# Banks of PSUM taken in the order given back, and a tick's masks placed ahead of its scores, in a sparse-attention and mixture-of-experts kernel

## The chip, the cores and the metric

The kernel runs on one core of one Trainium2 chip. The metric is the device time of one execution in microseconds (us). Three runs of the kernel before took 524.56, 526.11 and 528.07 us, so the median is 526.11 us.

## What is computed

Block-sparse attention (4 batches, 8 heads, 768 positions, 64 wide, blocks of 32) is followed by a mixture of 8 experts that sends every token to one expert. Cut to the core:

```python
scores = scale * np.matmul(q, k.transpose(0, 1, 3, 2))
mask = np.abs(blk_i - blk_j) <= 1                      # neighbours
mask |= first or last block, as a row or as a column   # dense rows and shared columns
mask |= three sampled blocks for each row of blocks
attn = softmax(np.where(mask, scores, -1e9))
x = (attn @ v) as (3072 tokens, 512)
logits = x @ w_gate + modality_bias[modality_id]
e_idx, gate_w = argmax(logits), softmax(logits) at e_idx
out[tokens of e] = gate_w * (relu(x @ w1[e]) @ w2[e])
```

## The kernel before, in words

The attention is cut into items. A dense item `("d", b, pr)` is the first and last block of queries of one batch and one pair of heads against all 24 blocks of keys. A sparse item `("s", half, m, n, b)` is one block of queries of one batch and all heads against 8 blocks of keys. There are 16 dense and 88 sparse items.

Every item passes through steps, each named by a letter: S scores (TensorE; `dense_scores`, L386, and `scores`, L536, which makes the scores of two sparse items, one for each batch), M maximum and mask (VectorE; `dense_max`, L399 and L400, and `masked`, L544), X exponential (ScalarE; L408, L409, L552), T transposes (TensorE; L418, L561), A copy of the transposes out of PSUM (mostly ScalarE; L425, L566), W and V the weighing of the values (TensorE; L437 for dense, L583 the shared blocks, L592 the own blocks; `sum_rows`, L576, the sums of the exponentials), O the division (VectorE; L444 to L446, L454), Y transposes of a finished tile of 128 tokens (L599, copied by ScalarE in L601) and G the gate (TensorE L609, read by VectorE in L612).

The loop runs in ticks. In tick t a step takes the item t minus the step's `LAG`; within a tick the steps are written out in the order of the string `ORDER`. Between the steps `hook(0)` to `hook(7)` put in other work: loads on SP's queue, copies of keys on GpSimd, routing on VectorE, and the first two groups of experts (`early_groups`). All five engines follow the order in which this code is written. In the first 14 ticks a list of tokens (`START`) sets it instead. After the attention, from about 237 us on, groups of 256 tokens run through the experts (`first_layer` L776 to L778, `second_layer` L791 to L793).

PSUM has 8 banks of 128 x 512 f32. Each result of TensorE takes one by calling `bank()`. Before, the pool handed them out in rotation: the n-th call gets the bank of call n - 8, and TensorE's first write to it waits until the last reader of that earlier holder is done. A holder lives for a very different time: the transposes of T until the copy two statements on, the bank of W from W over V to the last instruction of O, and the two banks of `scores` over the masks of two ticks.

Of the kernel before, what the change touches and what calls it, by code (L numbers as in the profile page):

```python
# [60 lines left out]
ORDER = 'OXTSMGVAYW'  # L61
# [28 lines left out]
def attention_moe(ctx, tc, kD, qD, qH, v0, v1, blocks, modality, w_gate, bias, w1, w2, out):  # L90
# [33 lines left out]
    with ExitStack() as actx:  # L124
# [3 lines left out]
        psum = actx.enter_context(tc.tile_pool(name="psum", bufs=8, space=PSUM))  # L128

        def bank():  # L130
            return psum.tile([P, 512], F32, name="bank")
# [81 lines left out]
        for _ in range(WARM):  # L213
            nc.tensor.matmul(warm[:, 0:P], lhsT=onesb, rhs=onesb, start=True, stop=True)

# [120 lines left out]
        def rank(t0_, t1_):  # L336
# [15 lines left out]
            nc.vector.tensor_tensor(cnt, cnt, rk[:, 256:256 + E], ALU.add)  # L352
            yield
# [25 lines left out]
        def dense_scores(b, pr):  # L379
            q = qd[b // HB]  # L380
            s1, s2 = zip(*[(bank(), bank()[:, 0:256]) for _ in range(2)])
            for o, blocks_ in ((s1, slice(0, 16)), (s2, slice(16, 24))):
                for c in range(2):
                    for u in range(2):
                        r, col = slice(64 * u, 64 * u + 64), 64 * (u ^ c)
                        nc.tensor.matmul(o[c][col:col + 64, :], lhsT=q[r, b % HB * NPAIR + pr + c], rhs=kd[b][r, pr // 2, blocks_, c * 32:c * 32 + 32],  # L386
                                         start=True, stop=True, tile_position=(64 * u, col))
            return zip(s1, s2)
# [8 lines left out]
        def dense_max(b, pr, s1, s2):  # L397
            nm2 = small.tile([P, 2], F32, name="nm2")
            nc.vector.tensor_reduce(nm2[:, 0:1], s1, axis=AX.X, op=ALU.max, negate=True)  # L399
            nc.vector.tensor_reduce(nm2[:, 1:2], s2, axis=AX.X, op=ALU.max, negate=True)  # L400
            nb_ = small.tile([P, 1], F32, name="nb_")
            nc.vector.tensor_scalar(nb_, nm2[:, 0:1], nm2[:, 1:2], 0.125, ALU.min, ALU.mult)
            return s1, s2, nb_

        def dense_exp(b, pr, s1, s2, nb_):
            a = work.tile([P, 768], F32, name="a", bufs=5)
            sm = small.tile([P, 2], F32, name="sm", bufs=6)
            nc.scalar.activation(a[:, 0:512], s1, AF.Exp, bias=nb_, scale=0.125, accum_out=sm[:, 0:1])  # L408
            nc.scalar.activation(a[:, 512:768], s2, AF.Exp, bias=nb_, scale=0.125, accum_out=sm[:, 1:2])  # L409
            return a, sm  # L410
# [10 lines left out]
        def dense_copy(b, pr, tps, sm):  # L421
            at = ad[0]
            ad.append(ad.pop(0))
            for k0, k1, tp in tps:
                (nc.vector.tensor_copy if (b, pr) in DENSE_DVE else nc.scalar.copy)(at[:, k0:k1, :].rearrange("p a b -> p (a b)"), tp[:, 0:(k1 - k0) * P])  # L425
            rt = small.tile([P, 1], F32, name="su", bufs=6)
            nc.vector.tensor_scalar(rt, sm[:, 0:1], sm[:, 1:2], 1e-9, ALU.add, ALU.add)
            nc.vector.reciprocal(rt, rt)
            return at, rt
# [19 lines left out]
        def dense_out(b, pr, o, rt):  # L449
            for u in range(2):  # L450
                col = 64 * (u ^ pr % 2)
                r = slice(col, col + 64)
                dst = xrs[-1, b // HB][64 * (b % HB):64 * (b % HB) + 64, (2 * pr + u) * D:(2 * pr + u + 1) * D]
                nc.vector.tensor_scalar(dst, o[r, 0:D], rt[r], None, ALU.mult)  # L454

# [84 lines left out]
        def masked(m, n, b, sp):  # L540
            y = work.tile([P, 512], F32, name="y", bufs=3).rearrange("p (u k) -> p u k", u=2)
            mn = small.tile([P, 2], F32, name="mn", bufs=4)
            for u in range(2):
                nc.vector.tensor_tensor_reduce(  # L544
                    y[:, u, :].rearrange("p (s f) -> p s f", s=8), sp[u][:, b * 256:(b + 1) * 256].rearrange("p (s f) -> p s f", s=8),
                    smask[:, 2 * m + 1 + n, :].unsqueeze(2).broadcast_to([P, 8, 32]), -0.125, 3.0e38, ALU.add, ALU.min, mn[:, u:u + 1])
            return y, mn
# [16 lines left out]
        def copied(n, b, tp, at):  # L564
            eng = nc.vector.tensor_copy if 2 * n + b in EVAC_DVE else nc.scalar.copy
            eng(at[:, :, n, :], tp.rearrange("p (x q) -> p x q", q=32))  # L566

# [28 lines left out]
        def turned(xr):  # L596
# [4 lines left out]
            nc.scalar.copy(xT.rearrange("p r t -> p (r t)"), tp)  # L601
            return xT

        def gate(tau, xT):
# [7 lines left out]
            nc.vector.tensor_tensor(lgs[tau - tau % 2][:, tau % 2, :], tp[:, 0:E], btok[:, tau, :], ALU.add)  # L612

# [189 lines left out]
        def early_groups():  # L803
# [21 lines left out]
            def columns(g):  # L825
                for n in range(2):
                    if now["column"] == 2 * g + n and now["gather"] > g:
                        column(g, n, bank())
# [20 lines left out]
            for k in range(4):  # L849
# [6 lines left out]
                relu(k, o)  # L856
            o = [bank() for _ in range(2)]
# [11 lines left out]
            for t in range(2):  # L869
                give(0, t, o[t])  # L870
            while now["column"] < 4:
# [9 lines left out]
            for k in range(4):  # L881
                relu(k, o[k])
            o = [bank() for _ in range(2)]
# [8 lines left out]
            for t in range(2):  # L892
                give(1, t, o[t])
            while not ready[2]:
# [5 lines left out]
            piece_numbers(bank())  # L900
# [129 lines left out]
        def choose(i):  # L1030
# [54 lines left out]
            yield from rows_of(tp, 2, gi_e[i], si_e[i])  # L1085
            ready[i] = True
# [8 lines left out]
        def finish():  # L1095
# [69 lines left out]
            yield from rows_of(tp, NCOL, gi, si, False)  # L1165
            ready[NEAR] = True
# [104 lines left out]
        def do(op, it):  # L1271
# [29 lines left out]
            else:  # L1301
# [20 lines left out]
                elif (n, b) == (1, HB - 1):  # L1322
# [7 lines left out]
                    elif op == "O":  # L1330
                        new_tile(m, half)
                        divide(st.pop(it), banks.pop((m, half))[:, 0:H], slice(0, P), H, xrs[m, half])
# [44 lines left out]
        hp, op, xp = [bank() for _ in range(4)], [bank() for _ in range(2)], [bank() for _ in range(2)]  # L1377
# [57 lines left out]
```

## Time and profile before

| | |
|---|---|
| median of 3 runs | 526.11 us |
| profiled execution, device time | 527.7 us |
| its span in the profile | 526.0 us |
| TensorE busy (matmuls) | 499.9 us, 95% |
| VectorE busy | 390.6 us, 74% |
| ScalarE busy | 341.0 us, 65% |
| GpSimd busy | 300.9 us, 57% |

In the profile PE is TensorE, PEld its weight loads, DVE is VectorE, ACT is ScalarE, POOL is GpSimd and SP the engine whose queue issues most transfers. Each row of a timeline gives the start in us from the span's start, the duration in us, then the engine, the line, the operation, what it writes and reads, and the number of instructions merged in it; a bracket at the end says how long the engine was idle before and what ended that. The 1.7 us between 526.0 and 527.7 lie outside of the instructions.

### The profile page before, as it was taken

To read this page: it belongs to the slowest core of one execution; us is meant where nothing else is said; L and a number is where in the kernel's file an instruction comes from. 1 tells how busy PE (TensorE), PEld (TensorE's weight loads), DVE (VectorE), ACT (ScalarE), POOL (GpSimd) and SP (SyncE) were. 2 spreads that over 40 slices of the span, in tenths; PEclk is the share of its full clock that TensorE was granted. 3 is DMA by queue.
4 is the path that set the end of the run, shared out by engine and by line. 5 is a ranking of instruction groups with operands and counts; after the bars stand their busy time and mean duration, and the time that the engine had idled before them with its cause. 6 is when DMAs were issued, how large, how long until landed. Compare 5 with 4: busy or idle time off the path is not lost.

```text
span 526.0 us, 18869 instructions
## 1 busy us (share of the span) xinstructions
PE 499.9 (95%) x7170; PEld 419.7 (80%) x7170; DVE 390.6 (74%) x1125; ACT 341.0 (65%) x777; POOL 300.9 (57%) x534
## 2 busy tenths in 40 slices
PE   7899898998999999889999999999999999999994
PEld 5577676776777777679898998989989899898983
DVE  7875776777877989975995757696776967869671
ACT  3679786886987998961564545464654646546471
POOL 3558763865466888454348742654746548465412
PEclk9989999998999999999999999999999999999997
DMA  7985987868855668968478884857759577585750
GB/s 279 326 232 156 227 248 240 244 175 255 217 178 151 190 203 242 267 195 273 160 242 304 294 272 148 304 184 264 261 183 306 179 259 254 194 305 186 263 196 23
DMA packets 49698, 119.40 MB, mean 227 GB/s; under 512 B 8512, under 2 KB 8896, under 8 KB 49600
## 3 DMA queue, kind: packets, MB, share of 16 engines
q1 hardware_dynamic: 44656, 105.00, 64.4%
q0 software_dynamic: 4944, 13.11, 6.7%
q8 instruction: 58, 0.95, 0.8%
q14 instruction: 40, 0.33, 0.2%
HBM read 105.50 MB, written 12.85 MB: 225 GB/s over the span
## 4 chain that ended last, share of the span: by engine, by line
PE 69%; DMA 14%; DVE 6%; SPq 5%; issue 3%; ACT 2%; POOL 1%; POOLq 0%; DVEq 0%; ACTq 0%
PE bank L776 8%; PE bank L778 8%; PE bank L777 8%; PE bank L793 7%; PE bank L792 7%; PE bank L791 7%; DMA slot<-x_d,gq 6%; PE bank L536 6%; PE bank L561 5%; PE bank L592 3%; PE bank L583 2%; DMA slot<-v 2%; DMA slot<-w 2%; DMA slot<-kD 2%; PE bank L609 2%
## 5 line engine op out<-in xcount | busy, mean ns | idle before, releaser
L728 DVE TENSOR_TENSOR slot<-slot 128x1024 fp32r<-128x1024 f32 x96 | 114.8, 1225 | 45.2 <-ACT slot L724 45.0
L748 POOL DMA_INDIRECT slot<-x_d,gq x72 | 94.5, 1313 | 76.3 <-DVE slot L755 57.0
L724 ACT CAST slot<-slot 128x1024 fp32r<-128x1024 f32 x104 | 106.3, 1047 | 40.0 <-PE bank L777 30.3
L776 PE MATMUL bank<-slot 128*128 128x256 f32 x384 | 107.2, 279 | 0.0
L777 PE MATMUL bank<-slot 128*128 128x256 f32 x384 | 106.3, 277 | 0.0
L778 PE MATMUL bank<-slot 128*128 128x256 f32 x384 | 106.3, 277 | 0.0
L552 ACT ACTIVATE a<-y,mn 128x256 f32<-128x256 f32 x176 | 88.8, 514 | 5.3 <-DVE mn L544 4.5
L793 PE MATMUL bank<-slot 128*128 128x512 f32 x200 | 78.9, 395 | 0.0
L792 PE MATMUL bank<-slot 128*128 128x512 f32 x200 | 78.7, 393 | 0.1
L791 PE MATMUL bank<-slot 128*128 128x512 f32 x200 | 78.4, 392 | 0.0
L777 PEld LDWEIGHTS bank<-slot 128*128 128x128 f32 x384 | 72.3, 188 | 0.4
L776 PEld LDWEIGHTS bank<-slot 128*128 128x128 f32 x384 | 72.1, 188 | 0.6
L778 PEld LDWEIGHTS bank<-slot 128*128 128x128 f32 x384 | 72.1, 188 | 0.0
L544 DVE CUSTOM_DVE_ANT_1 y<-bank,smask 128x256 f32<-128x256 f32 x176 | 66.4, 416 | 3.4 <-PE bank L536 3.0
L484 POOL COPY slot<-slot 128x128 f32 x264 | 64.9, 296 | 0.0
L566 ACT COPY at<-bank 128x512 f32<-128x512 f32 x88 | 50.8, 579 | 9.4 <-PE bank L561 9.4
L506 POOL TENSOR_SCALAR slot<-slot 32x1024 f32<-32x1024 f32 x40 | 41.8, 1045 | 25.6 <-issue 10.8
L561 PE MATMUL bank<-ident,a 128*128 128x128 f32 x352 | 53.2, 284 | 2.5 <-issue 2.5
L536 PE MATMUL bank<-slot,q_raw 64*32 64x256 f32 x1408 | 50.5, 387 | 2.1 <-DMA q_raw<-qH 1.9
L783 ACT ACTIVATE slot<-bank 128x512 fp32r<-128x512 f32 x48 | 28.7, 598 | 35.3 <-PE bank L778 32.5
L784 DVE SCALAR_TENSOR_TENSOR slot<-bank,slot 128x512 fp32r<-128x512 f32 x48 | 32.3, 690 | 20.5 <-ACT slot L783 20.5
L792 PEld LDWEIGHTS bank<-slot 128*128 128x128 f32 x200 | 37.6, 188 | 8.9 <-DVE slot L728 0.8
(299 smaller groups left out, 869.6 us busy)
## 6 DMA issues: line engine op xcount, KB each, us to landing
slot<-w SPq DMA_DIRECT2D x105, 512.0 KB, 5.4
slot<-v SPq DMA_DIRECT2D x180, 128.0 KB, 4.0
q_raw<-qH SPq DMA_DIRECT2D x22, 256.0 KB, 4.5
x_d<-xr SPq DMA_DIRECT2D x22, 256.0 KB, 3.5
slot<-v SPq DMA_DIRECT2D x16, 256.0 KB, 4.9
slot<-kD SPq DMA_DIRECT2D x13, 256.0 KB, 4.4
slot<-v SPq DMA_DIRECT2D x4, 768.0 KB, 13.2
slot<-kD SPq DMA_DIRECT2D x3, 768.0 KB
```

What stands on the lines that cost most here:

```text
L536: nc.tensor.matmul(sp[u][32 * pr:32 * pr + 32, b * 256:(b + 1) * 256], lhsT=q[r, b * NPAIR + pr, n, :], rhs=kv[r, s0:s0 + 8, b, pr, :], st ...
L552: nc.scalar.activation(a[:, u, :], y[:, u, :], AF.Exp, bias=mn[:, u:u + 1], scale=-1.0, accum_out=total[:, u:u + 1])
L561: nc.tensor.transpose(tp[:, k:k + P], a[:, u, c * P:(c + 1) * P], ident)
L724: nc.scalar.copy(h, staged(n))
L728: eng.tensor_tensor(l[:, k:k + size], staged(n)[:, k:k + size], h[:, k:k + size].bitcast(F32), ALU.subtract)
L748: nc.gpsimd.indirect_dma_start(out=xq[0][:, 4 * t + k, :], out_offset=None, in_=table, in_offset=bass.IndirectOffsetOnAxis(ap=gq[:, k, 2 * ...
L776: nc.tensor.matmul(o, lhsT=h[:, fs], rhs=xh[g % 2][:, c, :], start=c == 0 and f % 2 == 0, stop=False)
L777: nc.tensor.matmul(o, lhsT=h[:, fs], rhs=xl[g % 2][:, c, :], start=False, stop=False)
L778: nc.tensor.matmul(o, lhsT=l[:, fs], rhs=xh[g % 2][:, c, :], start=False, stop=c == 3 and f % 2 == 1)
L791: nc.tensor.matmul(o, lhsT=hh[0][:, f, ts_], rhs=h[:, fs], start=f == 0, stop=False)
L792: nc.tensor.matmul(o, lhsT=hh[0][:, f, ts_], rhs=l[:, fs], start=False, stop=False)
L793: nc.tensor.matmul(o, lhsT=hl[f // 4][:, f % 4, ts_], rhs=h[:, fs], start=False, stop=f == 7)
```

## The change

Each bank now is a buffer of its own with a number. A list `unused` holds the numbers of free banks; `bank()` takes the one that has been in the list longest, and a new function `leave` puts a bank at the list's end. `leave` is called right behind the statement that writes out a holder's last reader. So a call gets the bank whose last reader was written out longest ago, whoever held it. TensorE's first write still waits for that reader. `ORDER` has M in front of S, so that a tick's masks give their two banks back ahead of the tick's scores taking two. The expert groups after the attention take the banks 0 to 7 by number.

```diff
-ORDER = 'OXTSMGVAYW'
+ORDER = 'OXTMSGVAYW'
...
-        psum = actx.enter_context(tc.tile_pool(name="psum", bufs=8, space=PSUM))
+        psum = actx.enter_context(tc.tile_pool(name="psum", bufs=1, space=PSUM))
+
+        unused, held = list(range(8)), {}
+
+        def take(n):
+            return psum.tile([P, 512], F32, name="bank", tag=f"bank{n}", bufs=1)
 
         def bank():
-            return psum.tile([P, 512], F32, name="bank")
+            n = unused.pop(0)
+            held[n] = take(n)
+            return held[n]
+
+        def leave(*banks_):
+            for n in [n for t in banks_ for n in held if held[n] is t]:
+                del held[n]
+                unused.append(n)
...
             nc.scalar.activation(a[:, 0:512], s1, AF.Exp, bias=nb_, scale=0.125, accum_out=sm[:, 0:1])
-            nc.scalar.activation(a[:, 512:768], s2, AF.Exp, bias=nb_, scale=0.125, accum_out=sm[:, 1:2])
+            nc.scalar.activation(a[:, 512:768], s2[:, 0:256], AF.Exp, bias=nb_, scale=0.125, accum_out=sm[:, 1:2])
+            leave(s1, s2)
...
             eng(at[:, :, n, :], tp.rearrange("p (x q) -> p x q", q=32))
+            leave(tp)
...
+            if b == HB - 1:
+                leave(*sp)
             return y, mn
...
-                        divide(st.pop(it), banks.pop((m, half))[:, 0:H], slice(0, P), H, xrs[m, half])
+                        o, rows = st.pop(it), banks.pop((m, half))
+                        divide(o, rows[:, 0:H], slice(0, P), H, xrs[m, half])
+                        leave(o, rows)
...
-        hp, op, xp = [bank() for _ in range(4)], [bank() for _ in range(2)], [bank() for _ in range(2)]
+        banks_ = [take(n) for n in range(8)]
+        hp, op, xp = banks_[0:4], banks_[4:6], banks_[6:8]
```

(`leave` stands in the same way behind the last reader of every other holder.) On all five engines the instructions and their order stay what they were: M issues on VectorE alone and S on TensorE alone, and `hook(4)`, which stands between the two, has no work in any tick. What changes is for which earlier instruction the first write to a bank waits. That is so at 200 of TensorE's instructions.

First place: TensorE, from the transposes ahead of the dense scores at 124.69 us of the trace to the sums (L576) behind them. The names are those of the tiles without numbers; a bracket names the engines whose progress the instruction waits for. Before:

```order
L386 MATMUL bank<-slot,qd 64x512 [waits Activation_49]
L386 MATMUL bank<-slot,qd 64x512
L386 MATMUL bank<-slot,qd 64x512 [waits DVE_49]
L386 MATMUL bank<-slot,qd 64x512
L386 MATMUL bank<-slot,qd 64x256 [waits DVE_49]
L386 MATMUL bank<-slot,qd 64x256
L386 MATMUL bank<-slot,qd 64x256 [waits Activation_49]
L386 MATMUL bank<-slot,qd 64x256
L576 MATMUL bank<-rexp,fold 32x8 [waits DVE_49]
```

And now, with the changed kernel's line numbers (L401 is L386 of before, L597 is L576):

```order
L401 MATMUL bank<-slot,qd 64x512 [waits DVE_49]
L401 MATMUL bank<-slot,qd 64x512
L401 MATMUL bank<-slot,qd 64x512 [waits Activation_49]
L401 MATMUL bank<-slot,qd 64x512
L401 MATMUL bank<-slot,qd 64x256 x2
L401 MATMUL bank<-slot,qd 64x256 [waits Activation_49]
L401 MATMUL bank<-slot,qd 64x256
L597 MATMUL bank<-rexp,fold 32x8 [waits DVE_49]
```

The third bank's wait for VectorE is gone: it was for a mask (L544) that had read this bank's earlier holder. The second bank now waits for a copy on ScalarE (L566), the fourth for another one (L601 of before).

Second place: TensorE, the gate (L609 of before, L631 now) ahead of the weighing of shared blocks at 121.50 us. Before:

```order
L609 MATMUL bank<-wg_raw,xT 64x8 x7
L583 MATMUL bank<-slot,at 64x64 [waits DMAHW1_49,DVE_49,Pool_49]
L583 MATMUL bank<-slot,at 64x64 [waits Activation_49]
L583 MATMUL bank<-slot,at 64x64 x14
L561 MATMUL bank<-ident,a 128x128 [waits PE_49]
```

Now:

```order
L631 MATMUL bank<-wg_raw,xT 64x8 x7
L604 MATMUL bank<-slot,at 64x64 [waits DMAHW1_49,Pool_49]
L604 MATMUL bank<-slot,at 64x64 [waits Activation_49]
L604 MATMUL bank<-slot,at 64x64 x14
L581 MATMUL bank<-ident,a 128x128 [waits PE_49]
```

The weighing no longer waits for VectorE, because the gate one instruction group earlier has taken over that bank, and with it the wait for the division (L446) that read it.

The last reader of the earlier holder, for the banks whose wait the text speaks of:

| first write (time in the trace) | last reader, before | last reader, now |
|---|---|---|
| scores L536, second bank, 97.57 | exponential L409 | copy L566, the one after it |
| gate L609, 121.50 | L444 of the division | L446 of the division |
| dense scores L386, second bank, 124.69 | gate's addition L612 | copy L566 |
| the same, third bank, 127.91 | masks L544 | an earlier copy L566 |
| sums L576, 128.97 | mask L544, the last of its pair | mask L544, the one before it |
| transposes L561, 130.94 | copy L601 | mask L544, the last of its pair |
| scores L536, first bank, 132.13 | L444 of the division | L446 of the division, as the second bank before |
| dense scores L386, second bank, 136.68 | mask L544 | copy L601 |
| scores L536, second bank, 203.99 | L444 of the division | L446 of the division |

## Rows read from the trace of the kernel before

**Rows 1.** The page: the span, and busy time of each engine with its share

```profile
span 526.0 us, 18869 instructions
PE 499.9 (95%) x7170; PEld 419.7 (80%) x7170; DVE 390.6 (74%) x1125; ACT 341.0 (65%) x777; POOL 300.9 (57%) x534
```

**Rows 2.** Busy us by stretch: us, engines' busy us, TensorE's granted clock, DMA share, GB/s

```profile
0.00:237.00 237.00, 218.66 (x5272) 166.64 (x5272) 187.43 (x849) 188.54 (x586) 151.56 (x408) 0.98 0.77 223
237.00:515.00 278.00, 277.45 (x1885) 250.66 (x1885) 201.01 (x275) 150.98 (x190) 147.05 (x125) 1.00 0.70 238
```

**Rows 3.** Waits of PE, 70 to 240 us: waited for, us in total, times, longest

```profile
PE bank L592 <- DMA slot<-v: 2.3, 2, 1.7
PE bank L386 <- DVE mn L544: 2.1, 1, 2.1
PE bank L386 <- DMA slot<-kD: 1.4, 1, 1.4
```

**Rows 4.** Timeline, all engines, 123 to 133 us (columns as told above)

```profile
123.96 2.61 DVE L375 TENSOR_SCALAR lhs<-iota_f,rlo,code 128x128 f16<-128x128 f32 x1
...
124.67 0.57 ACT L566 COPY at<-bank 128x512 f32<-128x512 f32 x1
124.69 1.09 PE L386 MATMUL bank<-slot,qd 64*64 64x512 f32 x8
...
125.13 0.58 ACT L601 COPY xT<-bank 128x512 f32<-128x512 f32 x1
...
127.44 0.41 DVE L544 CUSTOM_DVE_ANT_1 y<-bank,smask 128x256 f32<-128x256 f32 x1
...
127.91 1.13 PE L386 MATMUL bank<-slot,qd 64*64 64x256 f32 x8 [2.13 <-DVE mn L544]
...
128.97 0.29 PE L576 MATMUL bank<-rexp,fold 128*32 128x8 f32 x8
...
129.10 1.91 PE L592 MATMUL bank<-slot,at 128*32 128x64 f32 x64
...
131.08 0.69 DVE L446 TENSOR_TENSOR xr<-bank,rt 128x512 f32<-128x512 f32 x1 [1.34 <-PE bank L592]
...
132.13 1.09 PE L536 MATMUL bank<-slot,q_raw 64*32 64x256 f32 x32
```

**Rows 5.** Busy us by stretch, as rows 2: around TensorE's slow and idle stretches

```profile
57.00:61.10 4.10, 2.96 (x112) 1.92 (x109) 2.58 (x12) 3.64 (x12) 1.46 (x2) 1.00 1.00 202
61.10:64.50 3.40, 3.40 (x86) 2.63 (x87) 2.36 (x11) 3.04 (x10) 3.40 (x11) 1.00 1.08 249
...
127.90:131.30 3.40, 3.39 (x82) 2.46 (x83) 0.89 (x5) 1.60 (x7) 0.00 (x0) 0.50 0.85 232
...
201.00:205.00 4.00, 3.75 (x128) 2.98 (x128) 3.77 (x20) 4.00 (x13) 3.81 (x13) 1.00 0.91 296
```

**Rows 6.** Timeline at the banks with new waits: 97, 121, 137 and 204 us

```profile
97.47 0.60 ACT L566 COPY at<-bank 128x512 f32<-128x512 f32 x1
...
97.57 1.18 PE L536 MATMUL bank<-slot,q_raw 64*32 64x256 f32 x32
...
121.15 0.69 DVE L446 TENSOR_TENSOR xr<-bank,rt 128x512 f32<-128x512 f32 x1
...
121.50 0.64 PE L609 MATMUL bank<-wg_raw,xT 128*64 128x8 f32 x16
...
136.56 0.60 ACT L601 COPY xT<-bank 128x512 f32<-128x512 f32 x1
...
136.68 1.54 PE L386 MATMUL bank<-slot,qd 64*64 64x512 f32 x16
...
138.24 1.08 PE L592 MATMUL bank<-slot,at 128*32 128x64 f32 x64
...
203.99 1.09 PE L536 MATMUL bank<-slot,q_raw 64*32 64x256 f32 x32
...
204.17 0.69 DVE L446 TENSOR_TENSOR xr<-bank,rt 128x512 f32<-128x512 f32 x1
```

## Prediction for the changed kernel

> **What bounds the kernel now.** I read the busy times by stretch first, then TensorE's waits in the attention, then the timeline around the one wait that belongs to a bank.
>
> The span is 526.0 us and TensorE is busy for 499.9 of them [rows 1]; the profiled execution took 527.7 us, 1.6 above the median of the runs shown. The idle time is not spread evenly. From 237 to 515 us TensorE is busy for 277.45 of 278 us at the full granted clock; from 0 to 237 us it is busy for 218.66, so 18.3 us are idle there [rows 2]. Two things follow. Behind 237 us nothing can be gained, because a bank that comes sooner meets a full engine. And what the attention gains or loses is passed on to the end nearly whole.
>
> Of the 18.3 us the change can reach only what a bank holds up. In the list of TensorE's waits from 70 to 240 us the longest entries are transfers and one single wait of 2.1 us: dense scores (L386) for a mask (L544) [rows 3]. That is the only large one that ends with the reader of a bank. The rest are for data: values, keys, copied transposes. So rotation holds TensorE up for long once in this stretch, not in every tick.
>
> **The one wait, and what replaces it.** The timeline shows the place [rows 4]. The first eight matmuls of L386 start at 124.69 us. VectorE then spends 2.61 us in one instruction of L375 from 123.96 us, so its masks come late; the mask of 127.44 us ends at 127.85 us, and the second eight matmuls, whose bank it had read, start at 127.91 us after 2.13 us of idle time.
>
> After the change the second bank waits for the copy of 124.67 + 0.57 = 125.24 us, so the first eight matmuls end near 125.24 + 1.09 = 126.33 us instead of 125.78. The third bank is free by then, and the fourth, read by L601 until 125.13 + 0.58 = 125.71 us, is too. All sixteen took 1.54 us in a later place at full clock [rows 6], so the second eight end about 126.33 + (1.54 - 1.09) = 126.8 us.
>
> What is late next: the sums (L576). Their bank now comes from the mask that ends at 127.85 us, so they start about 127.90 us and not at 128.97; that is 1.07 us sooner, and TensorE is still idle for about 127.90 - 126.8 = 1.1 us. The wait is cut in half, not removed.
>
> Behind it stands L592, which took 1.91 us here and 1.08 us at 138.24 us [rows 4, 6]. The reason is the clock: from 127.9 to 131.3 us the granted clock was 0.50, the lower of the two levels (1.2 against 2.4 GHz), right behind the 2.13 us of idle time [rows 5]. From 57 to 61.1 us TensorE was idle for 4.10 - 2.96 = 1.14 us, and the stretch behind it ran at 1.00 [rows 5]. The idle time that I expect is of that second size, so I take the full clock: L592 from 127.98 to 129.06 us instead of 131.01. The division (L446), which started 0.07 us behind it at 131.08 us, starts at 129.13 and ends at 129.82 us; the next scores (L536) wait for this division's bank before and after, and came 0.36 us behind its end (131.77 to 132.13), TensorE being busy with transposes until then. They come at about 130.1 us, **2.0 us sooner**. If the clock falls all the same, L592 ends at 127.98 + 1.91 = 129.89 us and the scores come about 1.2 us sooner. I take 2.0 and keep 1.2. The upper bound for this place is the whole 2.13 us of idle time plus the slow half of L592, 1.91 - 1.08 = 0.83 us, about 3.0 us.
>
> **The waits that the change adds.** The front of the list is now set by when a holder was given back in the program's text, and that need not be when its reader is done. Four places carry it.
>
> At 97 us the second bank of L536 waits for a copy that ends at 97.47 + 0.60 = 98.07 us; TensorE came to these scores at 97.57 us and to the second bank within 0.1 us [rows 6]. Cost 0.4 us, in a stretch where TensorE has little idle time. I take it whole.
>
> At 121 us the gate (L609) waits for the division that ends at 121.15 + 0.69 = 121.84 us instead of starting at 121.50 [rows 6]. Cost 0.34 us, but it is hidden: it moves the dense scores above, whose second bank is not free before 125.24 us anyway. I take nothing; without that cover it costs its 0.34 us.
>
> At 137 us the second bank of L386 waits for L601, until 136.56 + 0.60 = 137.16 us; TensorE came to the first bank at 136.68 us and to the second some 0.06 us later [rows 6]. Cost 0.4 us. Behind it stand L576 and L592, for which VectorE's division waits. I take it whole.
>
> At 204 us the second bank of L536 waits for the division that ends at 204.17 + 0.69 = 204.86 us, and TensorE was there right behind 203.99 [rows 6]. That is 0.86 us. From 201 to 205 us VectorE is busy for 3.77 of 4 us [rows 5], so it sets the pace and TensorE has to wait for it soon after in any case. The bounds are 0 and 0.86; I take 0.3, nearer the lower end for that reason.
>
> The other moved waits are for readers done before TensorE arrives, or smaller than the four. The M in front of S costs nothing by itself: the one issues on VectorE and the other on TensorE, so both queues stay as they are; it only lets the scores take a bank that the masks of that tick gave back. Nothing is added in DMA, in instructions or in bytes. The banks of the expert groups taken by number meet holders long finished; the busy 277.45 us cover that, and without this cover it is one wait at the first group.
>
> **Sum.** -2.0 + 0.4 + 0 + 0.4 + 0.3 = -0.9 us. Against the profiled execution that is 527.7 - 0.9 = 526.8 us; against the median of the runs, 526.11 - 0.9 = **525.2 us**. A measurement of this kernel can tell a change from none at about 1%, some 5.3 us, so I forecast no change.
>
> **The rivals.**
>
> *A. The gain is taken back before 237 us.* The 2.0 us are won at 132 us, and 105 us of attention follow in which VectorE and transfers also set the pace; two waits of L592 for values take 2.3 us [rows 3]. If these transfers go out no sooner, TensorE only waits longer there. Against it: SP issues these loads once the weighing has freed their buffers, and that moves with TensorE. Time: 526.1 to 526.5 us.
>
> *B. The new waits win: slower.* The place is 204 us and the ticks behind it. It decides if the 0.86 us there are not slack, since VectorE at 3.77 of 4 us has no room to catch up, and if the clock at 128 us falls as before. Then -1.2 + 0.4 + 0.34 + 0.4 + 0.86 = +0.8 us, or 526.9; with nothing left of the gain, +2.0 us, or 528.1 us.
>
> *C. The clock falls at a new place.* A slow stretch lasts 3.4 us here and its work takes up to twice as long, so each costs at most about 1.7 us [rows 5]. One of them instead of the one that goes would give 526.11 + 2.0 + 1.7 = 529.8 us at worst, and it takes three to be slower by 1%. Against it: the new waits are all below the 1.14 us after which the clock stayed up. The Trainium skill, "TensorE: Matmul & The Clock Gate", section on psum-queue depth-cycling, speaks for it: short idle times from cycling through PSUM banks made the clock of another kernel go up and down.
>
> *D. More than forecast is won.* If the masks of 127 us also come sooner, or later ticks lose waits that are too short to show in the list, the bound of 3.0 us with 0.8 from places that I cannot name gives 522.3 us.
>
> The Trainium skill, "Perfetto Trace Analysis", section Matmuls, asks that independent groups rotate through the banks so that the copies out of one overlap the next. By that rule the rotation taken away would cost; by the rows both orders use all 8 banks, and the sum goes by the rows.
>
> **How the numbers follow.** The forecast (0.5 to 2.5 us won) has 0.45, A 0.25, B 0.18, C 0.05, D 0.07. The range runs from D's 522.3 us to C's single slow stretch, cut a little below its worst case, at 529.3 us; it also takes in the distance between the runs shown, 524.56 to 528.07. For faster by over 1% (below 520.8 us) the bound of 3.0 us is not enough, so a part of D alone, 0.06; for slower by over 1% (above 531.4 us) several slow stretches of C or far more of B, 0.07; within 1%, 0.87.
>
> **What would show it.** In the profile after, the wait of L386 (L401) for a mask should be gone from TensorE's list, and one of about 1 us should stand at the sums (L597). The granted clock behind it should be 1.00. Scores at 97, 137 and 204 us should show short waits for a copy or a division. TensorE should still be full behind the attention, and the attention's end should be 0.5 to 1.5 us sooner. I am wrong if many short waits for banks appear in every tick, if the slow stretch at 128 us stays or comes elsewhere, or if the first group of experts waits for its banks.

## The result and the profile after

The changed kernel is slower, by little: 528.47 us against 525.23 us (medians of 22 executions each), ratio 1.0058 with an interval from 1.0032 to 1.0083, about +3.0 us. One of its executions took 1835.63 us and is left out of the ratio. The forecast was 525.2 us and no change. The time lies within the range, and within the 1% that was called no change, but its interval excludes no change, on the other side of the -0.9 us.

The profiled execution was the fastest of its 22, 522.74 us with a span of 521.0 us. So this one trace cannot show the loss as a longer span, only as a place. The page's span and busy times, and the busy times by stretch, to be read beside [rows 1, 2]:

```profile
span 521.0 us, 18864 instructions
...
PE 499.7 (96%) x7170; PEld 419.4 (80%) x7170; DVE 385.3 (74%) x1125; ACT 339.9 (65%) x777; POOL 299.8 (58%) x534
...
0.00:237.00 237.00, 224.56 (x5353) 173.21 (x5353) 187.62 (x862) 190.74 (x589) 156.39 (x411) 0.99 0.76 230
237.00:515.00 278.00, 274.81 (x1825) 246.21 (x1821) 197.66 (x263) 148.57 (x187) 142.39 (x122) 1.00 0.68 232
```

In front of 237 us TensorE is idle for 12.4 us instead of 18.3. Behind it, where it was full to 0.55 us, it is idle for 3.2 us. TensorE's waits from 237 to 515 us (columns as in [rows 3]) name the place:

```profile
PE bank L799 <- DVE gq L765: 2.1, 1, 2.1
PE bank L355 <- DVE oh L325: 0.5, 1, 0.5
PE bank L814 <- ACT slot L806: 0.4, 1, 0.4
```

L799 is the first layer of the first group of experts behind the early ones, and the wait is for a bank. The timeline there:

```profile
278.34 0.48 PE L763 MATMUL bank<-gf,ident 128*32 128x38 f32 x32
...
278.76 0.68 DVE L819 COPY slot<-bank 128x512 f32<-128x512 f32 x1
...
279.56 0.28 PE L799 MATMUL bank<-slot 128*128 128x256 f32 x1
...
281.48 0.38 DVE L765 TENSOR_SCALAR gq<-bank,q_f 128x152 int32<-128x152 f32 x1 [2.04 <-remote]
...
281.91 0.38 PE L799 MATMUL bank<-slot 128*128 128x256 f32 x1 [2.07 <-DVE gq L765]
```

L763 writes the piece numbers (which rows the later gathers fetch) into one bank, and VectorE's L765 reads them. It starts 281.48 - 278.82 = 2.66 us behind the last of these matmuls, though it had nothing else to do for 2.04 us. The expert groups now take the banks 0 to 7 by number, the piece numbers stand in bank 0, and the group's first accumulator (`hp[0]`) is bank 0. So TensorE does seven matmuls into other banks and then stands still.

Two statements ahead of the prediction were wrong, as the two programs show when each bank's first write is matched with its earlier holder.

First, the kernel before did not rotate strictly. Of 380 takings of a bank only 44 took that of the call eight earlier; the earlier holder was 3 to 15 calls back. So the banks already came in another order than that of the calls. The table of last readers did come from the real programs.

Second, TensorE's instructions do not all keep their order. At thirteen places of this first group another matmul stands than before, since their order is fitted to the banks when the program is built. Before, behind the piece numbers:

```order
L740 MATMUL bank<-gf,ident 32x38 x15
L776 MATMUL bank<-slot 128x256 [waits Activation_49]
L777 MATMUL bank<-slot 128x256 [waits DVE_49]
L778 MATMUL bank<-slot 128x256 [waits Pool_49]
L776 MATMUL bank<-slot 128x256
L777 MATMUL bank<-slot 128x256
L778 MATMUL bank<-slot 128x256
L776 MATMUL bank<-slot 128x256 [waits PE_49]
```

And now (L799 to L801 are L776 to L778 of before):

```order
L763 MATMUL bank<-gf,ident 32x38 x15
L799 MATMUL bank<-slot 128x256 [waits Activation_49]
L800 MATMUL bank<-slot 128x256 [waits DVE_49]
L801 MATMUL bank<-slot 128x256 [waits Pool_49]
L799 MATMUL bank<-slot 128x256
L800 MATMUL bank<-slot 128x256
L801 MATMUL bank<-slot 128x256
L799 MATMUL bank<-slot 128x256 [waits Activation_49]
L799 MATMUL bank<-slot 128x256 [waits DVE_49]
```

The last row is the wait for L765.

### The profile page after: what moved, and what is told of

It is laid out like the page before. It is cut to its first block, busy times and chain, and to the rows that moved or that the text cites. A ratio compares the mean times of both kernels' runs of the same rounds, so it can differ in the third digit from the quotient of the medians.

```text
span 521.0 us, 18864 instructions
## 1 busy us (share of the span) xinstructions
PE 499.7 (96%) x7170; PEld 419.4 (80%) x7170; DVE 385.3 (74%) x1125; ACT 339.9 (65%) x777; POOL 299.8 (58%) x534
## 4 chain that ended last, share of the span: by engine, by line
PE 50%; DMA 16%; POOL 9%; issue 8%; DVE 7%; ACT 4%; SPq 3%; POOLq 2%; another core or an unknown queue 0%; DVEq 0%; ACTq 0%
POOL slot L771 7%; PE bank L554 7%; DMA slot<-x_d,gq 6%; PE bank L581 6%; DMA out<-slot,si 5%; PE bank L799 4%; PE bank L801 4%; PE bank L800 4%; PE bank L816 3%; PE bank L815 3%; PE bank L814 3%; PE bank L613 3%; PE bank L604 3%; POOLq L976 2%; DMA slot<-kD 2%
## 5 line engine op out<-in xcount | busy, mean ns | idle before, releaser
L771 POOL DMA_INDIRECT slot<-x_d,gq x72 | 93.4, 1297 | 77.6 <-DVE slot L778 58.3
L799 PE MATMUL bank<-slot 128*128 128x256 f32 x384 | 107.3, 279 | 2.1 <-DVE gq L765 2.1
L801 PE MATMUL bank<-slot 128*128 128x256 f32 x384 | 106.3, 277 | 0.0
L799 PEld LDWEIGHTS bank<-slot 128*128 128x128 f32 x384 | 72.1, 188 | 2.8 <-DVE gq L765 2.3
L801 PEld LDWEIGHTS bank<-slot 128*128 128x128 f32 x384 | 72.1, 188 | 0.0
L806 ACT ACTIVATE slot<-bank 128x512 fp32r<-128x512 f32 x48 | 27.1, 599 | 40.4 <-PE bank L801 39.1
L581 PE MATMUL bank<-ident,a 128*128 128x128 f32 x352 | 52.1, 280 | 0.9 <-ACT a L423 0.5
L554 PE MATMUL bank<-slot,q_raw 64*32 64x256 f32 x1408 | 50.3, 382 | 2.3 <-DMA q_raw<-qH 1.7
L807 DVE SCALAR_TENSOR_TENSOR slot<-bank,slot 128x512 fp32r<-128x512 f32 x48 | 30.6, 686 | 26.8 <-ACT slot L806 25.5
```

What stands on the lines that cost most here:

```text
L554: nc.tensor.matmul(sp[u][32 * pr:32 * pr + 32, b * 256:(b + 1) * 256], lhsT=q[r, b * NPAIR + pr, n, :], rhs=kv[r, s0:s0 + 8, b, pr, :], st ...
L581: nc.tensor.transpose(tp[:, k:k + P], a[:, u, c * P:(c + 1) * P], ident)
L771: nc.gpsimd.indirect_dma_start(out=xq[0][:, 4 * t + k, :], out_offset=None, in_=table, in_offset=bass.IndirectOffsetOnAxis(ap=gq[:, k, 2 * ...
L799: nc.tensor.matmul(o, lhsT=h[:, fs], rhs=xh[g % 2][:, c, :], start=c == 0 and f % 2 == 0, stop=False)
L801: nc.tensor.matmul(o, lhsT=l[:, fs], rhs=xh[g % 2][:, c, :], start=False, stop=c == 3 and f % 2 == 1)
```

## The experiments

Four groups of four kernels, each group on one chip together with the kernel before. Four theories stand in what was expected of them: A, the bank of the piece numbers at the first group of experts costs the time; B, the attention's new waits do; C, banks given back in the order of the code but free later do; D, short waits at banks only take the place of others. A ratio is always to the kernel before on that chip; 0.19% is 1 us. In the four groups it rests on 10 to 12 executions of the kernel, but on 6 in e5_after and e14_after and on 4 in e8_third. "Lag" is worked out from each trace: the start of VectorE's read of the piece numbers less the end of their last matmul. "Gap" is TensorE's idle time for that read, among the first 60 matmuls behind it.

| kernel | chip | ratio | interval | lag, us | gap, us |
|---|---|---|---|---|---|
| first comparison, after | - | 1.0058 | 1.0032 to 1.0083 | 2.65 | 2.07 |
| e1_after | A | 1.0001 | 0.9958 to 1.0045 | 0.46 | none |
| e2_rqlast | A | 1.0032 | 0.9993 to 1.0072 | 0.46 | none |
| e3_rqshared | A | 1.0012 | 0.9977 to 1.0047 | 0.46 | none |
| e4_before | A | 0.9988 | 0.9952 to 1.0024 | 0.44 | none |
| e5_after | B | 1.0101 | 1.0045 to 1.0157 | 2.72 | 2.14 |
| e6_table | B | 0.9989 | 0.9952 to 1.0026 | 2.70 | none |
| e7_second | B | 1.0073 | 1.0017 to 1.0129 | 2.72 | 1.57 |
| e8_third | B | 1.0339 | 1.0245 to 1.0433 | 2.72 | none |
| e9_after | C | 1.0061 | 1.0021 to 1.0101 | 2.72 | 2.14 |
| e10_rqlast | C | 0.9995 | 0.9952 to 1.0039 | 2.71 | none |
| e11_rqshared | C | 1.0030 | 0.9987 to 1.0073 | 2.73 | 2.15 |
| e12_table | C | 0.9977 | 0.9940 to 1.0013 | 2.72 | none |
| e13_before | D | 1.0000 | 0.9968 to 1.0032 | 2.69 | none |
| e14_after | D | 1.0105 | 1.0059 to 1.0151 | 2.67 | 2.09 |
| e15_rqlast | D | 1.0015 | 0.9984 to 1.0046 | 2.66 | none |
| e16_table | D | 1.0010 | 0.9969 to 1.0050 | 2.68 | none |

### The first group's bank, put in and taken out (chip A)

e1_after and e4_before are the two kernels as they are. e2_rqlast gives the expert groups the banks in the order in which they are free, so that the one of the piece numbers comes last:

```diff
-        banks_ = [take(n) for n in range(8)]
+        banks_ = [take(n) for n in unused]
```

e3_rqshared is the kernel before with the piece numbers in the bank that the group takes first:

```diff
-            piece_numbers(bank())
+            shared.append(bank())
+            piece_numbers(shared[0])
...
-        hp, op, xp = [bank() for _ in range(4)], [bank() for _ in range(2)], [bank() for _ in range(2)]
+        hp, op, xp = [shared[0]] + [bank() for _ in range(3)], [bank() for _ in range(2)], [bank() for _ in range(2)]
```

> The changed kernel once more, for a second trace and more times. Theory A (the first group of experts): TensorE waits 2 to 2.5 us in the changed group of matmuls behind the piece numbers (L763), because the bank that they leave is the first hidden bank of group 2; the ratio to before is 1.003 to 1.006 and the wait of the first layer (L799) for gq (L765) stands in this trace too. Theory B (the attention): the waits for banks at 97, 137 and 204 us cost the time; the ratio is the same, but the wait in the first group is short or absent here, and the attention takes 2 to 3 us longer than in a copy of before.

> The changed kernel with one line other: the expert groups take the banks in the order of the list of free ones, so the bank of the piece numbers goes to the last of the eight and not to the first. The attention is untouched. Theory A: no wait of L799 for gq, TensorE full from the attention's end on, 2 to 2.5 us faster than the changed kernel, ratio to before 0.998 to 1.002. Theory B: as slow as the changed kernel, 1.003 to 1.006.

> The kernel before with its own way of giving banks and its own ORDER, but the piece numbers are written into a bank that the first hidden bank of group 2 then uses. Its attention is that of before. Theory A: a wait of 2 to 2.5 us of the first layer (L777) for gq, ratio to before 1.003 to 1.006. Theory B: no difference, 0.998 to 1.002.

> A copy of the kernel before, for a second trace of its attention and as the measure of what a comparison can tell: ratio 0.997 to 1.003 by both theories. Theory A: the attention ends within 1.5 us of where it ends in the changed kernel's traces on average; theory B: 2 to 3 us sooner.

All four are the same within their intervals, and the changed kernel itself shows no loss (1.0001). Theories A and B both expected one, and the wait that A expected in e1_after and e3_rqshared did not come. The reason stands in the timeline of e1_after: the same program, the same bank, but the read is early.

```profile
280.99 0.48 PE L763 MATMUL bank<-gf,ident 128*32 128x38 f32 x32
...
281.94 0.38 DVE L765 TENSOR_SCALAR gq<-bank,q_f 128x152 int32<-128x152 f32 x1
...
282.21 0.54 PE L799 MATMUL bank<-slot 128*128 128x256 f32 x2
```

L765 starts 0.47 us behind L763, and TensorE goes on without a gap. So this group tells nothing against the first group's bank; its traces, all with an early read, show no wait.

### The order of the attention's banks, changed (chip B)

A second suspect was the attention: "given back in the order of the code" is not "free in that order". A late holder is one whose last reader ends behind the next write to its bank. With each kernel's pairing of banks laid over three traces with the attention of before, the pairing of before has none, and that of the changed kernel has them at 7 to 10 places, by 2.2 to 3.8 us in sum. A kernel can have none on its own traces, since the write has waited there; but over the traces of after and e1_after, too, the pairing of before has none. e6_table takes the banks from a table, the pairing with the smallest such sum (0.3 to 1.1 us), and has e2_rqlast's edit:

```diff
-            n = unused.pop(0)
+            n = order_.pop(0)
+            unused.remove(n)
```

e7_second and e8_third take the second or the third of the free banks (1 in this edit of e7_second is 2 in e8_third):

```diff
-            n = unused.pop(0)
+            n = unused.pop(min(1, len(unused) - 1))
```

> The changed kernel once more, as it is. Theory C (written order): a bank that was given back in the order of the code is not a bank that comes free in that order. With each kernel's table of holders laid over three traces of the kernel before (end of the earlier holder's last reader less the start of the first write behind it), the holders of the kernel before never end after the write, and those of the changed kernel do at 7, 10 and 8 places, by 2.2, 2.7 and 3.8 us in sum, most of it where the earlier holder is read by the division on VectorE. Theory C expects +1 to +3.8 us over before (ratio 1.002 to 1.007), as in the first comparison (1.0058). Theory D (absorbed): short waits at banks take the place of other waits, and the true difference is nothing; it expects 0.998 to 1.002, as in the second comparison (1.0001).

> The changed kernel with the bank of each call from a table: the pairing of calls and earlier holders that makes the sum of late holders over five traces smallest, and the expert groups' banks in the order in which they are free. Late holders over the three traces of before: 0.3, 0.3 and 1.1 us, as many holders that end just ahead of the write as in the kernel before (16 to 20). Theory C expects the time of before (ratio 0.997 to 1.001), and e5_after 1 to 3.5 us above it. Theory D expects e5_after and e6_table to be the same within 1 us. Neither expects a gain over before of more than 1.5 us.

> The changed kernel, taking the second of the free banks in the list instead of the first (the first where there is only one). Late holders over traces of the changed kernel and of before: 58 to 65 places, 25 to 31 us in sum. Theory C: at least half of it is passed on to the end, +12 to +31 us (537 to 556 us). Theory D: most of it is taken up by waits that were there anyway (18 us of idle time in the attention), under +8 us.

> The same with the third of the free banks (the last where there are fewer). Late holders: 121 to 127 places, 76 to 85 us in sum. Theory C: +38 to +85 us, and per us of late holders as much as e7_second. Theory D: under +25 us.

Theory C's sizes fell. The 25 to 31 us of late holders in e7_second cost 0.73% of 528 us, 3.9 us, of which 1.57 us are the gap at the first group; the 76 to 85 us in e8_third cost 3.39%, 17.9 us. That is about 0.1 and 0.2 us for each us of late holders, so by this estimate the changed kernel's 2.2 to 3.8 us are worth 0.2 to 0.8 us. A late holder may delay TensorE once, so that the writes behind it come late themselves and wait less; that is an explanation and was not tested. Yet the changed kernel lost 1.01% here, no less than e7_second (the intervals overlap), and its trace has the late read and the gap again.

### The square of attention and first group (chip C)

> The changed kernel as it is, one corner of a square of four: banks of the attention in the order given back or not, and the bank of the piece numbers taken next by the first expert group or not. Theory A (first group): VectorE's read of the piece numbers (L765) came 0.45 us behind their last matmul in five traces and 2.65 to 2.72 us behind it in five others, of whatever kernel; only where the first expert group takes that same bank next does TensorE stand idle for the late 2.1 us. It expects e9_after over e10_rqlast, and e11_rqshared over before, by 2 to 2.6 us where the traces show the late read, and by nothing where they show the early one. Theory C (written order): the banks of the attention that are given back early in the code but come free late cost 0.3 to 3 us; it expects e9_after over e11_rqshared, and e10_rqlast over before, by that. Theory D: all four within 1 us.

> The changed kernel with the expert groups' banks in the order in which they are free, so that the piece numbers' bank is taken last: attention as in the changed kernel, first group as before. Theory A: the time of before, within 1 us. Theory C: 0.3 to 3 us over before and over e12_table.

> The kernel before with the piece numbers in the bank that the first expert group takes first: attention as before, first group as in the changed kernel. Theory A: 2 to 2.6 us over before where the read is late, the same where it is early. Theory C: the time of before, within 1 us.

> The kernel of e6_table once more: attention's banks by the pairing with the fewest late holders, first group as before. Theories A, C and D: the time of before, within 1 us (e6_table came 0.11% under before, interval from 0.48% under to 0.26% over). Were it 1.5 us or more under before, the pairing itself would be a gain.

The read is late in all four. TensorE's first layer in e11_rqshared, the kernel before with the shared bank:

```profile
286.42 0.39 PE L777 MATMUL bank<-slot 128*128 128x256 f32 x1 [2.15 <-DVE gq L743]
```

Only the two kernels with the shared bank have the gap. Taking it out of the changed kernel brings the ratio from 1.0061 to 0.9995; putting it into the kernel before gives 1.0030, where 2.15 us would be 1.0041. The interval of that 1.0030 takes in no change, so by the times alone this chip shows the loss in the changed kernel only. The attention's order by itself, e10_rqlast, shows no cost.

### The kernel before with a late read (chip D)

No trace yet showed the kernel before with the late read; one gap there would have upset theory A.

> The kernel before as it is, for a trace beside the others of its chip. Theory A: where the read of the piece numbers (L742 here) is 2.7 us late, TensorE still has no idle time in the first 60 matmuls behind them, since their bank is taken last by the first group. Were there a gap of 1.5 us or more, theory A would not explain the difference between the kernels.

> The changed kernel as it is. Theory A: where the read is late, a gap of 2.1 us at L799 and 2 to 6 us over e15_rqlast (it was 6.2 us with a standard error of 1.0, and some 0.5% less granted clock); where it is early, no gap and the same within 1.5 us.

> The changed kernel with the piece numbers' bank taken last by the expert groups. If the attention's order of banks gains, 1 us or more under before and under e13_before; if it does neither, within 1 us of them. In the two comparisons so far: +0.5 and -1.8 us, standard errors 0.9.

> The attention's banks by the pairing with the fewest late holders, the first group as in e15_rqlast. If late holders cost anything beyond the first group, 1 us or more under e15_rqlast; if not, within 1 us of it. In the two comparisons so far it came 2.3 and 1.6 us under before, standard errors 1.0 and 0.9.

The rows of e13_before: the piece numbers, their read, and the busy times (columns as in [rows 2]) in the 10 us from the piece numbers on:

```profile
281.16 0.48 PE L740 MATMUL bank<-gf,ident 128*32 128x38 f32 x32
...
284.33 0.38 DVE L742 TENSOR_SCALAR gq<-bank,q_f 128x152 int32<-128x152 f32 x1 [2.20 <-PE bank L778]
...
281.16:291.16 10.00, 10.00 (x114) 9.95 (x114) 7.32 (x16) 3.99 (x6) 6.86 (x7) 1.00 0.79 260
```

VectorE is just as late, and TensorE is full for all 10 us, because it writes to that bank last. The same 10 us in e14_after, and the wait:

```profile
278.50:288.50 10.00, 7.91 (x96) 7.66 (x96) 6.48 (x17) 4.00 (x5) 4.88 (x7) 1.00 0.86 281
...
282.09 0.38 PE L799 MATMUL bank<-slot 128*128 128x256 f32 x1 [2.09 <-DVE gq L765]
```

And in e15_rqlast, the changed kernel with one line mended:

```profile
279.26:289.26 10.00, 10.00 (x114) 9.95 (x114) 7.33 (x16) 3.43 (x5) 6.91 (x7) 1.00 0.76 251
```

With a late read the gap was there in the five traces in which the 8th matmul behind the piece numbers writes to their bank (`hp[0]`, 2.07 to 2.15 us), in the one where the 13th does (e7_second, `hp[2]`, 1.57 us), and in none of the other seven, where the 125th is the first. This settles where the gap comes from.

The size is settled in part. The changed kernel's four comparisons with a late read give 3.0, 5.3, 3.2 and 5.5 us, weighted by their intervals 3.7 us with a standard error of 0.5 (by the medians they are 3.2 to 5.4 us); the gap is 2.1. In one of the five traces, e9_after, the clock fell behind the gap:

```profile
284.50:288.30 3.80, 1.73 (x41) 1.25 (x39) 1.66 (x5) 2.13 (x3) 2.01 (x2) 1.00 0.83 225
288.70:292.10 3.40, 3.40 (x18) 3.40 (x17) 3.26 (x13) 0.01 (x1) 0.00 (x0) 0.50 0.54 196
```

The granted clock is 0.50 (the lower level, 1.2 of 2.4 GHz) for 3.4 us. The 100 matmuls from the 5,600th on took 15.4 us there, 13.8 us in the four others with the gap and 11.4 to 11.9 us in traces without it: 2.2 us for the gap and 1.6 more for the clock. The Trainium skill, "TensorE: Matmul & The Clock Gate", section on psum-queue depth-cycling, tells of another kernel in which frequent short idle times from cycling through PSUM's banks made the clock go up and down. Here there is one gap and not many, and the clock fell behind one of five. At one in five that is 0.3 us on average. Some 1.3 us of the loss stay open, between 0.3 and 2.3 us by two standard errors.

The clocks of all executions point to a part of it on one chip. On chip C the mean granted clock was 0.990 in e9_after and 0.995 in e10_rqlast, 12 executions each, and one stretch of 3.4 us at 0.50 takes 0.003 off such a mean; so there the clock may have cost more than 0.3 us. On B and D the changed kernel, with 6 executions each, has 0.993 and 0.994, and e6_table and e15_rqlast beside it 0.994 and 0.995, so nothing of the kind is shown.

## Why the prediction was wrong, point by point

**The step that failed** is the sentence on the expert groups: "The banks of the expert groups taken by number meet holders long finished; the busy 277.45 us cover that, and without this cover it is one wait at the first group." One holder was not long finished, the piece numbers, written right in front of the group. The cover was read as an average of the whole stretch. What was wanted is the last reader of that bank. The timeline of before has it:

```profile
285.97 0.48 PE L740 MATMUL bank<-gf,ident 128*32 128x38 f32 x32
...
286.90 0.38 DVE L742 TENSOR_SCALAR gq<-bank,q_f 128x152 int32<-128x152 f32 x1
```

It starts 0.45 us behind the matmuls, which looks harmless. With that lag it is harmless (e1_after). In the trace of after and on chips B to D the lag is 2.65 to 2.73 us, and the term is +2.1 us instead of 0. The failure itself was listed under what would make the forecast wrong, without a price.

**"Behind 237 us nothing can be gained"** was not contradicted, but a full engine can lose there, and whatever it loses goes to the end whole. That side was not priced, and no rival held it: B put the slower case into the attention.

**The main term, -2.0 us,** was right in mechanism, as far as one trace shows it, and wrong as an average. The wait of [rows 3, 4] came from the 2.61 us of L375. In 18 traces VectorE has such a long instruction there in 4: before, e5_after, e11_rqshared and e16_table. With the attention of before it gives the wait of L386 again, and the slow clock behind it (so it does with the pairing of e16_table, where the dense scores wait 1.9 us); rows of e11_rqshared:

```profile
122.39 2.88 DVE L375 TENSOR_SCALAR lhs<-iota_f,rlo,code 128x128 f16<-128x128 f32 x1
...
126.61 0.66 PE L386 MATMUL bank<-slot,qd 64*64 64x256 f32 x8 [2.40 <-DVE mn L544]
...
128.10:131.50 3.40, 3.40 (x52) 2.38 (x48) 2.89 (x8) 1.68 (x6) 0.00 (x0) 0.50 0.93 224
```

With the changed kernel's attention, in e5_after, it gives what was forecast: L401 runs through, a wait stands at the sums (L597), and the clock behind it stays at 1.00.

```profile
125.27 3.25 DVE L389 TENSOR_SCALAR lhs<-iota_f,rlo,code 128x128 f16<-128x128 f32 x1
...
126.29 1.79 PE L401 MATMUL bank<-slot,qd 64*64 64x512 f32 x16
...
129.86 0.25 PE L597 MATMUL bank<-rexp,fold 128*32 128x8 f32 x8 [1.78 <-DVE mn L562]
129.99 1.22 PE L613 MATMUL bank<-slot,at 128*32 128x64 f32 x64
...
130.60:134.00 3.40, 3.23 (x98) 2.34 (x87) 2.71 (x7) 2.23 (x8) 0.51 (x1) 1.00 0.99 252
```

The wait is 1.78 and not 1.1 us for two reasons. L389 ends 2.23 us behind the start of the dense scores, and L375 in [rows 4] ended 1.88 us behind it. And the prediction had the wait too short: it let all eight matmuls of 1.09 us wait for the copy until 125.24 us. But in the trace of before the fifth of them, the first in the second bank, starts at 125.17 us, so the copy costs 0.07 us, the sixteen end at about 126.3 us, and 127.90 - 126.3 = 1.6 us were to be expected. The 2.0 us do not hang on this, since the sums wait for the mask either way. But a gain of 2.0 us in 4 of 18 executions is 0.4 us on average. In the trace of after the place is without any wait. Without the change it would most likely have been so too: e3_rqshared, e4_before and e13_before, with the attention of before and no such long instruction, have no wait of L386 for a mask there. Rows of after:

```profile
121.27 1.52 PE L401 MATMUL bank<-slot,qd 64*64 64x512 f32 x16
122.72 0.25 PE L597 MATMUL bank<-rexp,fold 128*32 128x8 f32 x8
122.81 1.08 PE L613 MATMUL bank<-slot,at 128*32 128x64 f32 x64
```

**The new waits, +0.4, 0, +0.4 and +0.3 us,** were too large in sum. The 0.4 us at 137 us were a misreading: TensorE came to the second bank at 137.16 us, 0.48 and not 0.06 us behind the first, just when its reader ended. At 204 us the row of [rows 5] has ScalarE busy for all 4.00 us, so VectorE with 3.77 us was not the fullest engine there. In eight traces with the changed kernel's attention the gate (L631) waits 0.3 us for the division in four, scores (L554) wait 0.2 to 0.5 us for it in seven, and waits of 0.6 and 0.7 us of L554 and L401 for a copy stand in one trace each. Most of what the holders were late was taken up, as it was on a larger scale in e7_second and e8_third.

**The attention as a whole** went about as forecast. TensorE's idle time that ends with a bank's last reader, worked out from 20 to 237 us, is 3.9 us on average in five traces with the attention of before and 3.3 us in eight with the changed one. The 5,301st matmul, at the attention's end, starts at 236.1 us on average in the first (234.7 to 239.1) and at 234.9 us in the second (231.7 to 241.4). The spread is too wide to call that shown. In the times, e2_rqlast, e10_rqlast and e15_rqlast are within -0.05% and +0.32% of the kernel before; weighted by their intervals that is +0.8 us, with an interval from -0.3 to +1.9. So there is no gain to see, and a small loss in the attention, which would be a part of the open 1.3 us, is not excluded. Nor is there a gain in e6_table, e12_table and e16_table, whose pairing has the fewest late holders on these traces. No version is faster than the kernel before beyond its interval.

**Rival C**, a slow clock at a new place, came true as a side effect in e9_after, at a place that it did not name. The trace of after has a slow stretch at a new place too (0.50 from 215.3 to 218.7 us), but so has e13_before, at 218.6 us, so it need not come from the change. **B** had the sign, by the wrong place (its -1.2 us is, by the prediction's own rows, 131.01 - 129.89 = 1.1 us).

## What to carry to other kernels

When buffers are given numbers by hand at the border of two stages, look for the last reader of each number by name and put the freshest one last: a full engine behind the border hides nothing, and here one edit of one line took the gap away and, within the intervals of e10_rqlast and e15_rqlast, the loss with it. A wait that one profiled execution shows once, and whose cause is a coincidence of two engines, counts with the share of executions that have it. Before a term is put at nothing, ask what it becomes if a reader that was on time in this trace comes 2 us later in another.

## What the runs showed of the hardware

- **The same read came at two times.** VectorE started 0.44 to 0.46 us behind TensorE's last small matmul in five traces (the first of before and chip A) and 2.65 to 2.73 us behind it in thirteen, the same program among both (e1_after and e9_after). The times keep together by chip; why, no run here shows. The Trainium skill, "Perfetto Trace Analysis", section on TensorE's instructions, says that a matmul's end in a profile is estimated, and that its semaphore goes up when PSUM has taken the last bytes; so the lag may lie in either. The semaphore events kept with the traces narrow it. Behind other matmuls of this stretch the event stands 0.01 to 0.03 us after the recorded end. Behind the piece numbers it stands 0.41 us after it in e4_before and 2.67 us in e13_before, and there the events of the next four matmuls that signal follow within 0.37 us, though their recorded ends lie 1.4 us apart; the last two are on time again. So the signal of the piece numbers comes late, and the next signals stand behind it while matmuls go on. TensorE's own idle time of 2.1 us shows that the lag is no artefact of the record.
- **The same VectorE instruction beside the same copies of GpSimd took 0.33 or 2.61 us.** In e13_before L375 started 0.08 us behind the start of twelve copies and took 0.33 us; in before it started 0.11 us behind it and lasted to 0.15 us before their end ([rows 4] show L375). Rows of e13_before:

```profile
122.75 2.94 POOL L484 COPY slot<-slot 128x128 f32 x12
...
122.83 0.33 DVE L375 TENSOR_SCALAR lhs<-iota_f,rlo,code 128x128 f16<-128x128 f32 x1
```

  And of before:

```profile
123.85 2.87 POOL L484 COPY slot<-slot 128x128 f32 x12
```

  The other three long ones, in e5_after, e11_rqshared and e16_table, also started within 0.1 us behind the start of an instruction of GpSimd and lasted to about the end of such copies. What decides between the two, no run here shows. The Trainium skill, "SBUF — State Buffer", section on the two separate sides, has an exclusive lock between the two engines, for some VectorE instructions (those in a two-port mode or with two inputs in SBUF), that the first one keeps for its whole instruction. No run here shows whether L375 is one of these; if it is, the rule by itself gives a wait for one copy (0.28 us), and the long one lasted into the twelfth.
- **The clock goes with the spread on one chip and not on another.** Over the 35 executions of before on chip A (520.4 to 531.3 us) the time rises by 5.0 us for each 1% of granted clock lost, with a correlation of -0.72; one slow stretch of 3.4 us at 0.50 is 0.3%. On chips B and C the correlation is -0.58 and -0.40, and over the 29 executions on chip D (520.0 to 532.0 us) it is -0.08. So something else spreads the times too, and no run here shows what.
